# Regrouping the triangular inversions of a delta-rule kernel: groups of 2, 2, 4, 4, 4, 4, 4 chunks instead of 2, 4, 4, 4, 4, 4, 2

## The chip, the core and the metric

The kernel runs on one core of a Trainium2 chip. The metric is the device time of one launch in microseconds; the time before is 1050.36 us, the median of three runs. The engines are TensorE (PE, with PEld for its weight loads), VectorE (DVE), ScalarE (ACT), GpSimd (POOL) and SyncE (SP), whose queue issues all transfers.

## What is computed

A delta-rule attention over 4 batches, 8 heads, 768 tokens and 48 channels is followed by two feed-forward layers over 3072 tokens (384 to 2048 to 384), all in float32.

```python
def _attn_ref(q, k, v, beta):
    k_n = k / (np.linalg.norm(k, axis=-1, keepdims=True) + 1e-06)
    state = np.zeros((B, H, D, D))
    for t in range(S):
        kt, vt, bt = k_n[:, :, t], v[:, :, t], beta[:, :, t, None]
        y[:, :, t] = np.einsum('bhd,bhde->bhe', q[:, :, t], state)
        v_old = np.einsum('bhde,bhd->bhe', state, kt)
        state = state + bt[:, :, :, None] * np.einsum('bhd,bhe->bhde', kt, vt - v_old)
    return y
# layer 1: h = x @ w_in;  g = h if h >= 1, 0 if h <= -1, else (h+1)**2/4;  x = g @ w_out
# layer 2: h = x @ w_in;  g = max(h, 0)**2;                                out = g @ w_out
```

## The kernel before, in words

**Chunks, blocks, units.** The 768 tokens are cut into 24 chunks of 32 tokens; a chunk of all four batches fills 128 partitions. For the feed-forward layers, chunks are joined into blocks (`SIZES` = 2, 2, 3, 3, 3, 3, 3, 2, 3). A unit (L778) is one of 16 slices of 128 of the hidden dimension for one block: the first layer's nine matmuls (`hidden`, L616; three blocks of channels times three products of high and low halves), the relu steps on ScalarE and VectorE (L632 to L647), and, two units later (`LAG` = 2), the second layer's nine matmuls (`out1`). Blocks 0 and 1 have 256 columns, most later ones 384. Units are numbered through: block 0 is units 0 to 15, block 1 units 16 to 31.

**Slots.** Each unit has two slots; slot 2x stands after the first layer of unit x, slot 2x+1 after the second-layer matmuls of unit x-2. `put_a(n, slot, f)` places work ahead of what `put(n, slot, f)` places in the same slot. Every engine runs its own instructions in this written order, so a place in it is a place in the queue of each engine that the work uses.

**Chunk work.** For each chunk, `chunk_steps` gives Ks, Tr, Qs, Ku, Pu and Xt: five groups of 64 small matmuls each (L517 to L568) and a transposition, with a copy or a subtraction after each. Tr multiplies with the inverse of a 32 x 32 triangular matrix. The matrices come from `gram(c)` (L289): 64 matmuls of the chunk's keys with its keys and queries, then a multiplication with a mask (L318). The inversion works on a group of chunks at once, up to four (8 heads times 4 chunks fill the 32 x 32 transpositions). `tri(n, eng)` (L377) gives its parts: `begin`, one transposition by VectorE (L395, some 2.1 us); `pre`, nine small operations for norms and scaling, on ScalarE, VectorE and, for whole matrices, half of the last two on GpSimd (L425, L434), ended by a copy to the diagonal (L435); `steps`, a multiplication and an addition per row (L455, L456), on GpSimd, 30 rows; and `end`, a transposition back by VectorE (L459). There is one buffer for the matrix under inversion (`tx`).

**Groups 0 and 1.** They are inverted by halves (two 16 x 16 triangles, 14 steps), and the off-diagonal part is added on TensorE by `Ld` and `Dld` (`joined`, L468; 64 matmuls for a chunk each, L488 and L496), for which `save` keeps a copy and `rows` (L484) transposes half of the result. Group 0 (chunks 0, 1) is inverted by VectorE in the prologue. Group 1 (chunks 2 to 5) is inverted by GpSimd across the end of the prologue and the first units; grams 2 to 5 stand in the prologue, `rows1` in slot 3, Ld of chunks 2 and 3 in slot 5, `end1` behind it, Ld of chunks 4 and 5 in slot 7, Dld in slots 8 and 24. Chunks 2 and 3 take their chunk steps in slots 9 to 22.

**Later groups.** Group 2 begins with chunk 6: its grams stand in slots 9, 10, 12 and 15. For every group g from 2, `tri_put` (L946) places `begin` one slot after the group's last gram, `pre` three to a slot from the next, the steps from there evenly, and `end` one slot before the first Ks of the group's first chunk. The chunk steps of block n stand evenly in the 32 slots of block n-1, and the grams of the next group go between the steps of a group's first chunk (L922 to L942). That gives, for group 2: begin in slot 16, steps in slots 20 to 45, end in slot 48, first Ks in slot 49. `value(c)` is one GpSimd multiplication per chunk, five slots ahead of its Ks.

**Weights.** Block 0 also makes the weights ready: each of 32 tiles is loaded as 64-bit numbers and turned into two words' high and low halves: two operations of ScalarE (L170, L173, "bits"), one of VectorE (`make`, L180), a cast to the high half (`upper`, L214) and a subtraction for the low half (`lower`, L219). `between(f)` (L727) spreads them over units 0 to 13: two tiles a and b a unit. Tile a's cast is ScalarE's; tile b's is GpSimd's from unit 3. Two weight loads at most are under way, all on SP's queue, with the loads of chunks among them (L805 to L810). `load_kg` loads a gram's keys and queries into a ring of two buffers; the loads of chunks 4 and 5 stand ahead of all weights, those of 6 and 7 after weights 14 and 16.

Of the kernel before, what the change touches and what calls it, by code (L numbers as in the profile page):

```python
# [21 lines left out]
GROUPS = [2, 4, 4, 4, 4, 4, 2]  # L22
# [3 lines left out]
def kernel(  # L26
# [441 lines left out]
    def joined(n):  # L468
        if n == 0:
            l = wp.tile([P, 2, H, T], F32, tag=spare["l"], name="l")  # L470
            z = [wp.tile([P, 2, H, T], F32, tag=spare["z"], name="z")]
            d = wp.tile([P, GC * H, T2], F32, tag=spare["d"], name="d")
        else:
            l = ring.tile([P, GC, H, T], F32, tag="ld", bufs=1, name="l")
            z = [ring.tile([P, 2, H, T], F32, tag="raw", bufs=RAW, name="z") for _ in range(2)]
            d = ring.tile([P, GC * H, T2], F32, tag="raw", bufs=RAW, name="d")
# [250 lines left out]
    def between(f):  # L727
        a, b = tiles[2 * f:2 * f + 2]

        def part(x):  # L730
            if x == 0:
                if a is not None:
                    make(a)
                some(2)
            elif x == 1:
                if a is not None:
                    upper(a, nc.scalar.copy)
                if b is not None:
                    make(b)
                if last_low:  # L740
                    lower(last_low.pop(), V)
            elif x == 2:
                if b is not None:
                    upper(b, G.tensor_copy if f > 2 else nc.scalar.copy)
                    last_low.append(b)
                some(2)
            elif a is not None:
                lower(a, V)

        return part  # L750
# [45 lines left out]
    with tc.manual_schedule():  # L796
# [6 lines left out]
        for c in range(KG):  # L803
            load_kg(KQ + c)
        among = {1: lambda: load_kv(1), 8: lambda: load_kv(HEADS)}  # L805
        for x in range(NW - HELD):
            among.get(x, lambda: None)()
            load_w(order[x])
            if x in (14, 16):
                load_kg(KQ + KG + (x - 14) // 2)  # L810
# [27 lines left out]
        masks += [gram(c, late=2, eng=G) for c in range(KQ, KQ + KG)]  # L838
# [5 lines left out]
        after(value(0), ins)  # L844
        value(1)
        for c in range(HEADS):
            mask_of_head(c)
        go(masks)
# [6 lines left out]
        make(1)  # L855
# [4 lines left out]
        dld0(1)  # L860
        upper(1, nc.scalar.copy)
        whole_bits(4)
        make(2)
        lower(1, V)
        for c in range(GROUPS[1]):
            save1(c)
        upper(2, nc.scalar.copy)
        begin1()
        s0()
        t0()  # L870
        pre1[0]()
        whole_bits(5)
        whole_bits(6)
        s1()
        whole_bits(7)
        t1_()
        go(pre1[1:])
        steps1[0]()
        value(2)
        go(steps1[1:])  # L880
        lower(2, V)
        make(3)
        whole_bits(8)
        upper(3, nc.scalar.copy)
        make(4)
        lower(3, V)
# [4 lines left out]
        x0()  # L891
        upper(4, nc.scalar.copy)
        x1()
        lower(4, V)
        whole_bits(9)
# [13 lines left out]
        put_a(0, 7, lambda: ld1(2), lambda: ld1(3))  # L909
        put_a(0, 8, lambda: dld1(0), lambda: dld1(1))  # L910
        put_a(0, 24, lambda: dld1(2), lambda: dld1(3))
        for c, at_ in ((2, (9, 11, 12, 13, 14, 16)), (3, (15, 17, 18, 19, 20, 22))):
            def steps_of(c=c, box={}):
                if c not in box:
                    box[c] = chunk_steps(c)
                return box[c]
            for i, slot in enumerate(at_):
                put_a(0, slot, lambda i=i, g=steps_of: g()[i]())
# [3 lines left out]
        for c, slot in zip(range(GFIRST[2], GFIRST[3]), (9, 10, 12, 15)):  # L922
            ready[c] = slot
            put_a(0, ready[c], lambda c=c: gram(c))
        for n in range(2, NB):
# [12 lines left out]
            for i, (mark, s_) in enumerate(todo):  # L938
                slot = SL * (n - 1) + i * SL // len(todo)
# [94 lines left out]
```

## Time and profile before

| what | value |
|---|---|
| runs | 1049.24, 1050.36, 1055.89 us |
| the profiled execution | 1048.56 us, span 1046.8 us |
| TensorE busy | 993.8 us, 95% of the span |
| VectorE, ScalarE, GpSimd busy | 582.7, 476.1, 293.3 us |
| mean granted TensorE clock | 0.985 |
| first layer of unit 0 begins | 44.47 us |

The page cuts the span into 40 slices; a digit is tenths. A timeline line gives start, duration, engine, line, operation, tiles written and read, shapes and count; in brackets stands how long the engine had been idle before it and what it waited for. "Issue" is idle time in which the engine waited for nothing that the profile shows.

### The profile page before, as it was taken

What the parts mean: (1) busy time and instruction counts of PE and PEld (TensorE: products, weight loads), DVE (VectorE), ACT (ScalarE), POOL (GpSimd) and SP (SyncE); (2) the same over time, 40 slices, a digit from 0 to 9 for tenths busy, and PEclk for the clock granted to TensorE, in tenths of its full rate; (3) what the DMA queues carried; (4) which work ended last, traced back from release to release, by engine and by line L of the source; (5) the groups of instructions that cost most, each with busy time, mean ns of one, the idle gap of its engine ahead of it and who ended that gap; (6) DMA issues with size and microseconds to landing.
All of it is one profiled execution on the core that took longest, in us unless ns stands there. A gap on an engine that the chain in (4) does not pass through costs nothing.

```text
span 1046.8 us, 33713 instructions
## 1 busy us (share of the span) xinstructions
PE 993.8 (95%) x14824; PEld 949.9 (91%) x14824; DVE 582.7 (56%) x1066; ACT 476.1 (45%) x993; POOL 293.3 (28%) x434
## 2 busy tenths in 40 slices
PE   6669788999999999999999999999999999999998
PEld 5568688898999989999999999999999999999998
DVE  6766965765575566566545677543434343443333
ACT  3756454554554545535445554433333333333332
POOL 3611691492058119419500223110101011010000
PEclk9969899999999999999999999999999999999999
DMA  8776245441541542512111323010101010000000
GB/s 221 223 228 156 64 119 143 110 137 47 154 131 33 172 112 79 145 32 70 32 56 41 94 90 120 2 46 1 46 1 46 1 46 1 23 1 23 1 23 23
DMA packets 36051, 80.93 MB, mean 77 GB/s; under 512 B 4544, under 2 KB 18368, under 8 KB 35904
## 3 DMA queue, kind: packets, MB, share of 16 engines
q1 hardware_dynamic: 35904, 78.78, 25.7%
q8 instruction: 116, 1.90, 0.8%
q14 instruction: 31, 0.25, 0.1%
HBM read 63.03 MB, written 15.73 MB: 75 GB/s over the span
## 4 chain that ended last, share of the span: by engine, by line
PE 82%; DMA 8%; DVE 5%; issue 1%; ACT 1%; SPq 1%; POOL 0%; DVEq 0%; ACTq 0%; POOLq 0%
PE acc L606 36%; PE h L606 36%; DMA raw<-in_w_dram 6%; PE sps L568 2%; PE tr L537 2%; PE yy L523 2%; PE g L302 1%; PE yy L557 1%; PE ks L523 1%; DMA kqt<-in_kq_dram 1%; DVE gl L647 1%; DVE g L633 1%; DVE g L636 1%; DVE wl L180 1%; SPq L129 1%
## 5 line engine op out<-in xcount | busy, mean ns | idle before, releaser
L606 PE MATMUL h<-xh,w 128*128 128x384 f32 (+1 forms) x1632 | 320.3, 332 | 5.3 <-ACT r L632 2.6
L606 PEld LDWEIGHTS h<-xh,w 128*128 128x128 f32 x1632 | 272.4, 190 | 10.1 <-ACT r L632 3.1
L647 DVE TENSOR_TENSOR gl<-g,gh 128x384 fp32r<-128x384 f32 (+1 forms) x272 | 172.3, 633 | 136.8 <-ACT gh L645 131.2
L645 ACT CAST gh<-g 128x384 fp32r<-128x384 f32 (+1 forms) x272 | 134.5, 494 | 208.3 <-DVE g L636 92.9
L606 PE MATMUL h<-xl,w 128*128 128x384 f32 (+1 forms) x816 | 179.3, 328 | 1.3 <-DVE xl L594 1.3
L606 PE MATMUL acc<-gh,w 128*128 128x384 f32 (+1 forms) x864 | 168.5, 331 | 0.8 <-ACT gh L645 0.8
L640 DVE TENSOR_TENSOR g<-r 128x384 f32<-128x384 f32 x128 | 71.3, 557 | 158.5 <-ACT r L639 158.5
L606 PE MATMUL acc<-w,gh 128*128 128x384 f32 x768 | 155.7, 337 | 1.9 <-DVE e L655 1.9
L639 ACT ACTIVATE r<-h,zero 128x384 f32<-128x384 f32 x128 | 74.2, 580 | 167.5 <-PE h L606 167.5
L606 PEld LDWEIGHTS h<-xl,w 128*128 128x128 f32 x816 | 141.0, 190 | 2.0 <-DVE xl L594 2.0
L606 PEld LDWEIGHTS acc<-gh,w 128*128 128x128 f32 x864 | 137.2, 191 | 5.9 <-ACT gh L645 0.9
L606 PEld LDWEIGHTS acc<-w,gh 128*128 128x128 f32 x768 | 136.6, 188 | 2.2 <-ACT gh L645 2.2
L632 ACT ACTIVATE r<-h,one 128x384 f32<-128x384 f32 (+1 forms) x144 | 78.3, 544 | 96.4 <-PE h L606 95.8
L636 DVE SCALAR_TENSOR_TENSOR g<-r,g 128x384 f32<-128x384 f32 (+1 forms) x144 | 89.7, 623 | 42.2 <-ACT g L635 40.5
L633 DVE TENSOR_SCALAR g<-r 128x384 f32<-128x384 f32 (+1 forms) x144 | 60.1, 417 | 86.2 <-ACT r L632 85.1
L455 POOL TENSOR_TENSOR t<-tx,gm 128x58 f32<-128x58 f32 (+9 forms) x164 | 95.7, 583 | 24.2 <-DVE tx L429 8.1
L456 POOL TENSOR_TENSOR tx<-tx,t 128x58 f32<-128x58 f32 (+9 forms) x164 | 97.7, 596 | 12.4
L635 ACT ACTIVATE g<-g 128x384 f32<-128x384 f32 (+1 forms) x144 | 70.2, 488 | 55.0 <-DVE g L633 54.4
L697 POOL CAST xh<-x2r 128x1152 fp32r<-128x1152 f32 x8 | 9.4, 1172 | 293.4 <-PE h L606 246.1
L606 PE MATMUL acc<-gl,w 128*128 128x384 f32 (+1 forms) x432 | 91.3, 320 | 0.0
L606 PE MATMUL acc<-w,gl 128*128 128x384 f32 x384 | 88.1, 337 | 0.0
L606 PEld LDWEIGHTS acc<-gl,w 128*128 128x128 f32 x432 | 72.7, 191 | 0.0
(101 smaller groups left out, 846.7 us busy)
## 6 DMA issues: line engine op xcount, KB each, us to landing
raw<-in_w_dram SPq DMA_DIRECT2D x64, 384.0 KB, 3.8
kqt<-in_kq_dram SPq DMA_DIRECT2D x88, 192.0 KB, 4.1
kv<-in_kv_dram SPq DMA_DIRECT2D x24, 384.0 KB, 3.1
w2f<-wl SPq DMA_DIRECT2D x32, 192.0 KB, 4.0
w2r<-w2f SPq DMA_DIRECT2D x16, 384.0 KB, 3.1
x2r<-x SPq DMA_DIRECT2D x8, 576.0 KB, 4.3
out_dram<-e SPq DMA_DIRECT2D x24, 192.0 KB, 2.0
x<-e SPq DMA_DIRECT2D x18, 192.0 KB, 2.5
```

Source lines behind the costliest of these rows:

```text
L455: eng.tensor_mul(t, by.to_broadcast(shape), of.to_broadcast(shape))
L456: return eng.tensor_add(rest, rest, t)
L523: per_bh(lambda b, h, p, pd: nc.tensor.matmul(o[p, h], kqt[c][pd, b // 2, h, x * T:(x + 1) * T], st[pd, b // 2, h], start=h == 0, stop=x = ...
L606: nc.tensor.matmul(o, *((r, l) if swap else (l, r)), **flags)
L632: marks[0] = nc.scalar.activation(r, h, AF.Relu, bias=one)
L633: marks[1] = nc.vector.tensor_scalar(g, r, 2.0, 0.5, ALU.min, ALU.mult)
L635: nc.scalar.activation(g, g, AF.Square)
L636: nc.vector.scalar_tensor_tensor(g, r, -1.0, g, ALU.add, ALU.max)
L639: marks[0] = nc.scalar.activation(r, h, AF.Relu, bias=zero)
L640: marks[1] = nc.vector.tensor_mul(g, r, r)
L645: nc.scalar.copy(ghi, g)
L647: nc.vector.tensor_sub(glo, g, ghi.bitcast(F32))
```

## The change

Group 1 becomes chunks 2 and 3 alone, group 2 begins with chunk 4 and all later groups shift by two chunks; the last has four. Grams 4 and 5 leave the prologue; grams 4 to 7 stand in slots 1, 3, 9 and 11 of block 0. By the same rules group 2 then has begin in slot 12, steps in slots 16 to 31, end in slot 35, first Ks in slot 36 (the chunk steps of block 2 start four slots into block 1); group 3 has steps from slot 51 and its end in slot 71. Ld and Dld of the second pair of chunks are gone. In the prologue `begin1` and `pre1` stand earlier, the masks of chunks 2 and 3 come before `value(1)`. The loads of chunks 4 to 7 for the grams go among the weight loads. In `between`, both casts are GpSimd's in units 3 to 7 and both ScalarE's elsewhere.

```diff
-GROUPS = [2, 4, 4, 4, 4, 4, 2]
+GROUPS = [2, 2, 4, 4, 4, 4, 4]
...
-            l = ring.tile([P, GC, H, T], F32, tag="ld", bufs=1, name="l")
-            z = [ring.tile([P, 2, H, T], F32, tag="raw", bufs=RAW, name="z") for _ in range(2)]
+            l = ring.tile([P, 2, H, T], F32, tag="ld", bufs=1, name="l")
+            z = [ring.tile([P, 2, H, T], F32, tag="raw", bufs=RAW, name="z")]
...
+        copy = G.tensor_copy if 2 < f < 8 else nc.scalar.copy
...
-                    upper(a, nc.scalar.copy)
+                    upper(a, copy)
...
-                    upper(b, G.tensor_copy if f > 2 else nc.scalar.copy)
+                    upper(b, copy)
...
-        for c in range(KG):
-            load_kg(KQ + c)
-        among = {1: lambda: load_kv(1), 8: lambda: load_kv(HEADS)}
+        among = {
+            1: lambda: load_kv(1), 4: lambda: load_kg(KQ), 6: lambda: load_kg(KQ + 1),
+            8: lambda: load_kv(HEADS), 18: lambda: load_kg(KQ + 2), 20: lambda: load_kg(KQ + 3),
+        }
...
-            if x in (14, 16):
-                load_kg(KQ + KG + (x - 14) // 2)
...
-        masks += [gram(c, late=2, eng=G) for c in range(KQ, KQ + KG)]
...
+        go(masks)
         value(1)
         for c in range(HEADS):
             mask_of_head(c)
-        go(masks)
...
         make(0)
-        make(1)
+        begin1()
         whole_bits(3)
         upper(0, nc.scalar.copy)
         lower(0, V)
         dld0(0)
         dld0(1)
+        pre1[0]()
+        go(pre1[1:])
+        steps1[0]()
+        make(1)
...
+        value(2)
+        go(steps1[1:])
         whole_bits(7)
         t1_()
-        go(pre1[1:])
-        steps1[0]()
-        value(2)
-        go(steps1[1:])
...
         put_a(0, 5, lambda: ld1(0), lambda: ld1(1))
-        put_a(0, 7, lambda: ld1(2), lambda: ld1(3))
-        put_a(0, 8, lambda: dld1(0), lambda: dld1(1))
-        put_a(0, 24, lambda: dld1(2), lambda: dld1(3))
-        for c, at_ in ((2, (9, 11, 12, 13, 14, 16)), (3, (15, 17, 18, 19, 20, 22))):
+        put_a(0, 7, lambda: dld1(0), lambda: dld1(1))
+        for c, at_ in ((2, (9, 10, 12, 13, 14, 16)), (3, (15, 17, 18, 19, 20, 22))):
...
-        for c, slot in zip(range(GFIRST[2], GFIRST[3]), (9, 10, 12, 15)):
+        for c, slot in zip(range(GFIRST[2], GFIRST[3]), (1, 3, 9, 11)):
...
-                slot = SL * (n - 1) + i * SL // len(todo)
+                o = 4 if n == 2 else 0
+                slot = SL * (n - 1) + o + i * (SL - o) // len(todo)
```

## Rows read from the trace of the kernel before

**Rows 1.** The page, part 2: granted TensorE clock in 40 slices, in tenths.
```profile
PEclk9969899999999999999999999999999999999999
```

**Rows 2.** Windows of block 1 and after: length, engines' busy us, clock, DMA share, GB/s.
```profile
131.61:192.84 61.23, 56.01 (x1514) 51.48 (x1514) 36.18 (x71) 30.15 (x73) 26.56 (x43) 1.00 0.46 125
192.84:264.00 71.16, 69.78 (x1338) 63.95 (x1337) 47.59 (x84) 37.73 (x79) 41.78 (x66) 1.00 0.34 97
```

**Rows 3.** Waits of TensorE from 44 to 210 us: total, times, longest.
```profile
PE z L488 <- DVE g L633: 6.1, 1, 6.1
PE xt L591 <- ACT kv L561: 5.7, 2, 4.1
```

**Rows 4.** Timeline, end of group 1's inversion: VectorE, GpSimd, TensorE.
```profile
56.08 1.05 DVE L484 STREAM_TRANSPOSE d<-tx 128x512 f32<-128x512 f32 x1 [0.48 <-POOL tx L456]
...
55.78 0.26 POOL L456 TENSOR_TENSOR tx<-tx,t 128x28 f32<-128x28 f32 x1
...
57.27 1.90 PE L488 MATMUL z<-d,l 32*32 32x16 f32 x128 [6.11 <-DVE g L633]
```

**Rows 5.** Timeline of TensorE, prologue, Tr of chunk 0.
```profile
33.41 1.01 PE L537 MATMUL tr<-kv,gp 32*32 32x48 f32 x36 [2.56 <-issue]
```

**Rows 6.** Timeline of TensorE, units 3 to 6, and one gram's mask on VectorE.
```profile
64.74 0.98 PE L488 MATMUL z<-d,l 32*32 32x16 f32 x94
66.08 0.46 PE L488 MATMUL z<-d,l 32*32 32x16 f32 x34 [0.37 <-issue]
66.47 0.98 PE L606 MATMUL h<-xh,w 128*128 128x256 f32 x6
67.29 0.52 PE L606 MATMUL h<-xl,w 128*128 128x256 f32 x3
67.73 0.96 PE L496 MATMUL w<-gp,z 32*32 32x16 f32 x84
71.93 0.82 PE L496 MATMUL w<-gp,z 32*32 32x16 f32 x44 [3.24 <-issue]
...
82.40 0.95 PE L606 MATMUL h<-xh,w 128*128 128x256 f32 x6
...
78.18 0.69 DVE L318 TENSOR_TENSOR gp<-g,mask 128x512 f32<-128x512 f32 x1 [1.15 <-PE g L302]
```

**Rows 7.** Timeline: first layer of unit 8, then group 2's preparation, first and last step.
```profile
96.35 0.98 PE L606 MATMUL h<-xh,w 128*128 128x256 f32 x6
...
112.39 0.20 DVE L435 COPY tx<-st 128x32 f32<-128x32 f32 x1 [0.51 <-POOL tx L434]
...
114.94 0.41 POOL L455 TENSOR_TENSOR t<-tx,gm 128x30 f32<-128x30 f32 x1
...
160.14 0.26 POOL L456 TENSOR_TENSOR tx<-tx,t 128x30 f32<-128x30 f32 x1
```

**Rows 8.** Timeline of GpSimd, first and last step of group 5.
```profile
390.01 0.24 POOL L455 TENSOR_TENSOR t<-tx,gm 128x30 f32<-128x30 f32 x1 [1.14 <-DVE tx L434]
...
430.36 0.46 POOL L456 TENSOR_TENSOR tx<-tx,t 128x30 f32<-128x30 f32 x1
```

**Rows 9.** Timeline: end of group 2 on VectorE; TensorE: Tr after it, Pu of chunk 4.
```profile
165.15 2.22 DVE L459 STREAM_TRANSPOSE gp<-tx 128x1024 f32<-128x1024 f32 x1
...
169.57 0.88 PE L537 MATMUL tr<-kv,gp 32*32 32x48 f32 x64 [1.82 <-DVE kv L533]
...
142.84 0.88 PE L557 MATMUL yy<-kv,gp 32*32 32x48 f32 x64
```

**Rows 10.** Timeline of TensorE: a second layer after 4.1 us idle; Xt of chunk 4.
```profile
114.77 1.63 PE L606 MATMUL acc<-gh,w 128*128 128x256 f32 x6
...
147.76 0.55 PE L591 MATMUL xt<-ident,kv 128*128 128x128 f32 x3 [1.61 <-ACT kv L561]
```

**Rows 11.** Gram 7 on TensorE; the weight casts (ns min/median/max, first and last start).
```profile
79.30 1.10 PE L302 MATMUL g<-kqt 48*32 48x64 f32 x64
80.33 0.97 PE L606 MATMUL acc<-gh,w 128*128 128x256 f32 x6
...
L214 ACT CAST w<-wl x22: 494/511/519, 27.2 to 126.2; 128x384 fp32r<-128x384 f32 x22
L214 POOL CAST w<-wl x10: 704/718/827, 64.2 to 122.7; 128x384 fp32r<-128x384 f32 x10
```

More of the change, by code (lines that the diff above doesn't have):

```diff
@@ L860 @@
         dld0(1)
+        pre1[0]()
+        go(pre1[1:])
+        steps1[0]()
+        make(1)
         upper(1, nc.scalar.copy)
-        whole_bits(4)
-        make(2)
-        lower(1, V)
         for c in range(GROUPS[1]):
             save1(c)
-        upper(2, nc.scalar.copy)
-        begin1()
+        whole_bits(4)
+        lower(1, V)
         s0()
         t0()
-        pre1[0]()
         whole_bits(5)
@@ L874 @@
         s1()
+        value(2)
+        go(steps1[1:])
         whole_bits(7)
         t1_()
-        go(pre1[1:])
-        steps1[0]()
-        value(2)
-        go(steps1[1:])
+        make(2)
+        whole_bits(8)
+        upper(2, nc.scalar.copy)
+        make(3)
         lower(2, V)
[L882 to L886, printed above, removed]
         q1()
@@ L891 @@
         x0()
+        upper(3, nc.scalar.copy)
+        make(4)
+        x1()
+        lower(3, V)
         upper(4, nc.scalar.copy)
-        x1()
+        whole_bits(9)
         lower(4, V)
-        whole_bits(9)
         whole_bits(10)
```

## The prediction

> **What bounds the kernel now.** I read the page first. The granted clock is full in almost all of the 40 slices and falls only near the start [rows 1], and the windows after block 1 show TensorE busy for 69.78 of 71.16 us [rows 2]. So from there on TensorE is the bound, and every microsecond it idles or runs at the lower clock counts one for one. What can be won lies before: in block 1 TensorE is busy for 56.01 of 61.23 us [rows 2], and earlier it idles more. The view of waits, for TensorE from 44 to 210 us, names the two largest [rows 3]: 6.1 us before the first Ld matmuls of group 1, and 5.7 us in two waits of the transposition xt, 4.1 the longer. Then the timeline shows who is late at each.
>
> The first wait looks like the gain of this change: GpSimd ends the inversion of group 1 at 55.78 + 0.26 = 56.04, VectorE's transposition of its rows (L484) starts at 56.08, TensorE's Ld at 57.27 [rows 4]. But the same row says that VectorE had waited only 0.48 us for GpSimd. It was itself busy until 56.08 - 0.48 = 55.6 with the conversions and relu steps of units 0 and 1. An inversion that ends six microseconds sooner moves this place by half a microsecond and no more.
>
> **The change, part by part.** The sum is made against the profiled execution's own 1048.56 us (span 1046.8, 1.76 around it). The median of the three runs is 1050.36, so 1.8 us more; a difference within 1% (10.5 us) is about what a measurement of this kernel cannot tell from no change.
>
> *Prologue: 0.* Grams 4 and 5, two saves and the GpSimd masks of chunks 4 and 5 leave it; the inversion of group 1 begins earlier. The first layer of unit 0 hangs on another chain, inversion of group 0, Ld, Dld, chunk steps 0 and 1, and the grams stood in a time in which TensorE waits for that inversion. The stall of 2.56 us inside tr of chunk 0 [rows 5] lies on it. I count it as staying: two grams are 128 matmuls, and two such stalls, at 66.08 and 71.93, have 34 + 9 + 84 = 127 between them [rows 6], so the next ones fall on the same instructions as before. Bounds: -2.6 (the stall goes) to +1 (one more weight cast of 0.51 us on ScalarE [rows 11] ahead of unit 0, and its wait).
>
> *Units 0 to 5: -5.* Added ahead of L484 on VectorE: the masks of grams 4 and 5, 0.69 each [rows 6], less the 0.48 that it waited: +0.9. Removed: Ld of two chunks, 64.74 to 66.47, 1.73 us [rows 6]; part of the 3.24 us stall that ends at 71.93 [rows 6], because the Dld now stands half a unit earlier and the work between is less dense; and part of the half-rate time after it. Fully taken that is 0.9 - 1.7 - 3.2 = -4.1, and with 2 us of slow clock -6.2; I take -5. Grams 4 and 5 themselves run while TensorE waits for VectorE anyway. Bounds: -0.8 (only the Ld goes) to -9 (also the whole first wait). So unit 6 starts its first layer at 77.4 instead of 82.40 [rows 6].
>
> A row and a rule differ here. The 3.24 us are "issue": nothing that the profile shows was waited for. The Trainium skill, "Runtime: NRT & Kernel Launch", section "Instruction fetch mechanics", says that an engine's instructions come in blocks of 256, the next fetched while the current one runs, so that a boundary is mostly hidden. The spacing fits such blocks (a matmul and its weight load are two instructions), the hiding does not. By the rule nothing would stall again and this term would be -9, by the rows -5.
>
> *Group 2 on GpSimd: the new wait.* This is the part that decides. Today the gram of the last chunk of the group stands just before the first layer of unit 8 (96.35); VectorE has the last preparation at 112.59 (L435), and GpSimd steps from 114.94 to 160.40 [rows 7], with two weight casts among them. The end is due in slot 48, unit 24. After the change the same chain hangs on unit 6: last gram in slot 11, begin in slot 12, steps from slot 16, end in slot 35, first Ks in slot 36. The distance from that first layer to the last preparation is 112.59 - 96.35 = 16.2 us. No casts are in the way any more, since units 8 and later cast on ScalarE. The 30 steps took 40.8 us from 390.01 to 430.82 [rows 8] with one value product, so 41.5 with what else is issued beside them. End possible at 77.4 + 16.2 + 41.5 = 135.1.
>
> When would the others reach the end in slot 35? From the first layer of unit 6 at 82.40 to Ku of chunk 4 done, at 142.84, the old kernel took 60.4 us [rows 6, 9]. In that stretch two grams go (2.1), Dld of two chunks with its wait (some 3, an estimate from the 1.73 of their Ld), and the four steps of chunk 4 come behind the end (3.5): 51.8 us, so at 77.4 + 51.8 = 129.2. VectorE stands there 6 us before GpSimd is done. It waits in order, so all later relu steps wait behind it, then the Ks subtraction of chunk 4, and TensorE at the Tr of chunk 4. From the start of the end's transposition to a Tr took 165.15 to 169.57, 4.4 us [rows 9]; Tr, Qs and Ku are three more steps of about 0.87. So at 135.1 + 4.4 + 2.6 = 142.1 the kernel is where the old one was at 142.84 (first layers up to unit 18, Ku of chunk 4) [rows 9]: -0.7. Of the 5 us won and of ten slots' earlier start almost nothing is left; TensorE idles some 10 us.
>
> *Clock after it: +2.* After the 4.1 us wait of xt [rows 3] six matmuls of a second layer took 1.63 us [rows 10], against 0.95 for six of the same size at the full clock [rows 6]; that is 1.0 lost in a layer of nine matmuls, and some two layers pass before the clock is back. Bounds 0 to 3.
>
> *Block 1 afterwards: -3.4.* The end of group 2 no longer stands in front of Tr of chunk 6 (1.82 us of idle [rows 9]), and the wait of xt at 147.76 (1.61 us [rows 10]) falls into the time in which TensorE is held anyway. Bounds -3.4 to 0.
>
> *Two grams later: +2.1.* Blocks 2 and later have twelve grams where they had ten; one takes 1.03 us of TensorE (79.30 to 80.33 [rows 11]), and there TensorE is full. Nothing hides it. Bounds 2.1 to 2.3.
>
> *Group 3: +1.* Its steps stand from slot 51, its end in slot 71. At 61.23/16 = 3.83 us a unit in block 1 and about 4.1 in block 2 (71.16 us for some 17 units [rows 2]) that is 6.5 x 3.83 + 3.5 x 4.1 = 39 us, for 41 to 42 of GpSimd. It is late by 2 to 3 us; a unit's two layers cover most. Bounds 0 to 6. Groups 4 to 6 have 23 or more slots, 47 us: nothing.
>
> *Casts: 0.* The condition 2 < f < 8 takes units 3 to 7, five units and ten tiles; ten are on GpSimd today too [rows 11], spread over units 3 to 12. They move to a time in which GpSimd is idle, and ScalarE, which is then rid of them, gains 0.51 us a unit [rows 11]. Units 8 and 9 get two casts beside their weight bits; should ScalarE set the pace there, it costs 0.51 a unit.
>
> *Loads: 0.* The gram loads go behind weights 4, 6, 18 and 20 on SP's queue. The last two wait for buffers that grams 4 and 5 free in units 0 and 1, before the queue is there. The bytes are the same. The loads of grams 8 and 9 leave block 0. Bounds -0.6 to +2.
>
> Sum: -0.7 + 2 - 3.4 + 2.1 + 1 = +1.0, so 1049.6 us.
>
> **The rivals.** *A, the early gain stays.* The stall of 3.24 and more of the first wait go, the term of units 0 to 5 is -9, unit 6 starts at 73.4 and the end of group 2 is possible at 131.1: 1045.6, and 1043 with less slow clock. For it: VectorE's conversions of units 0 and 1 then no longer run beside GpSimd's steps. Against: VectorE's busy time before L484 and the two added masks. The page's rule named above leads here too.
>
> *B, the short window of group 3 decides, slower.* Place: VectorE's wait at slot 71. If GpSimd begins its steps only 2 us later than counted (value products and the preparation stand before it), VectorE is held for 5 us, the transposition and the way to Tr add 4.4, and the clock falls once more, 2: 9 to 11 instead of +1, about 1058. It decides as soon as the lateness exceeds what two layers cover, some 4 us. For it: 39 us against 41.5. Against: an end stands in the window after block 1 too, where TensorE idles 1.4 us in all [rows 2]; but there GpSimd had 29 slots.
>
> *C, nothing of it is on the path:* the wait of group 2 is not there because units 8 to 17 take 42 us or more. Then TensorE is not idle but slowed by as much; 1046 to 1052, and the time does not tell it from the forecast.
>
> **How the numbers follow.** Forecast with C 0.50, A 0.25, B 0.20, other 0.05. The range reaches from 1041 (A with the bound of the prologue) to 1060 (B), with little beyond. Faster by over 1% would need 1039.9: a part of A and of "other", 0.13. Slower by over 1%, from 1060.9: a part of B and "other", 0.12. Within: 0.75.
>
> **What would show it.** Right: L484 starts near 57, not near 50; the Ld follows it; unit 6 begins near 77; GpSimd steps group 2 from about 94 to 135; VectorE's transposition of the end (L459) is released by GpSimd, and TensorE's longest wait is Tr of chunk 4, 9 us or more, followed by a stretch at 1.2 GHz. Wrong: no wait for GpSimd at the end of group 2, steps in under 38 us, or a longer wait at group 3 than at group 2.

## The result, and the profile after

The changed kernel takes 1061.16 us, the median of six runs (1060.06 to 1066.14), against 1050.92 for six runs of the kernel before: a ratio of 1.0102, with a 95% interval of 1.0071 to 1.0132. It is slower by 1%. The prediction was 1049.6 with a range of 1041 to 1060: wrong in the number, in the sign and, by a little, in the range. The profiled execution took 1061.56 us (span 1059.8), so 13.0 more than that of before (by medians it is 10.2); the steps below are counted against these 13.0, the experiments by medians.

The page, parts 2 and 4: the granted clock, and the chain that ended last.

```profile
PEclk9988879999999999999999999999999999999999
...
PE 83%; DVE 8%; POOL 3%; issue 3%; ACT 2%; DMA 0%; SPq 0%; DVEq 0%; ACTq 0%; POOLq 0%
```

The clock is lower in slices 4 and 6 than in [rows 1] (8 and 7 against 9 and 9) and higher in slice 3 (8 against 6). GpSimd, which holds 0% of the chain on the page of the kernel before, now holds 3%.

Windows of the kernel after, cut at the first layers of units 0 and 6, at Tr of chunk 4 and at the end of block 1; the columns are those of [rows 2], VectorE's busy time being the third of the five.

```profile
47.48:81.52 34.04, 27.11 (x858) 24.42 (x858) 25.07 (x53) 24.79 (x59) 4.25 (x8) 0.85 0.62 194
81.52:147.47 65.95, 48.27 (x823) 43.64 (x817) 56.93 (x96) 32.93 (x80) 45.92 (x70) 0.83 0.38 102
147.47:198.69 51.22, 50.23 (x1396) 46.16 (x1396) 30.02 (x65) 24.40 (x59) 21.00 (x35) 0.95 0.42 119
```

The second window is where the time goes: TensorE works 48.27 of 65.95 us, at a mean clock of 0.83, and VectorE is busy for 56.93 of them. For the kernel before, the nearest window, from unit 6 to the start of Pu of chunk 4, shows:

```profile
82.40:142.84 60.44, 49.23 (x1272) 44.93 (x1264) 47.67 (x97) 32.43 (x80) 32.51 (x48) 0.92 0.36 95
```

There VectorE had 47.67 us of work with 97 instructions; now it has 56.93 with 96. The kinds are nearly the same, so the instructions became dearer. TensorE, on the other hand, runs 823 matmuls where it ran 1272: part of its work has moved behind this window.

Waits of TensorE in the kernel after, from 44 to 215 us (total, times, longest), to be held against [rows 3]:

```profile
PE yy L557 <- issue: 5.0, 2, 3.7
PE tr L537 <- DVE gp L459: 4.7, 1, 4.7
PE g L302 <- DVE gp L318: 3.9, 1, 3.9
...
PE xt L591 <- ACT kv L561: 1.1, 1, 1.1
```

The two waits of [rows 3] are gone or small. In their place stand the end of group 2 (L459), gram 5 waiting for gram 4's mask, and an issue stall of 3.7 us.

The first layers show where the 13.0 us arise (starts in us, from the timelines of TensorE in both profiles):

| first layer of unit | before | after | difference |
|---|---|---|---|
| 0 | 44.47 | 47.48 | +3.0 |
| 6 | 82.40 | 81.52 | -0.9 |
| 18 | 139.58 | 139.45 | -0.1 |
| 19 | 143.66 | 148.91 | +5.3 |
| 20 | 148.13 | 154.68 | +6.6 |
| 36 | 210.59 | 215.61 | +5.0 |
| 38 | 218.34 | 229.44 | +11.1 |
| 96 | 473.42 | 486.46 | +13.0 |

Three places lose: the prologue (3.0), the end of group 2 between units 18 and 20 (6.7), and the end of group 3 between units 36 and 38 (6.1). Units 0 to 5 win 3.9. Not all of the 6.7 and 6.1 is waiting: in both places the kernel after also runs two steps more, with one Xt less (in units 36 and 37 a Tr and a gram): some 1.5 us each time, an estimate from 0.82 us for a step, 1.03 for a gram and 0.3 for the Xt at the full clock.

**The prologue.** Timeline of the kernel after: VectorE, ScalarE and TensorE.

```profile
33.48 0.69 DVE L429 TENSOR_TENSOR tx<-gm,st 128x512 f32<-128x512 f32 x1
34.21 0.20 DVE L435 COPY tx<-st 128x32 f32<-128x32 f32 x1
...
34.43 0.52 DVE L180 SCALAR_TENSOR_TENSOR wl<-raw 128x384 int32<-128x384 int32 x1
35.03 0.51 ACT L214 CAST w<-wl 128x384 fp32r<-128x384 f32 x1 [5.70 <-DVE wl L180]
...
36.94 0.46 ACT L545 COPY u<-tr 128x384 f32<-128x384 f32 x1
```

The preparation of group 1 (to L435) now stands ahead of `make(1)` (L180) on VectorE. ScalarE comes to the cast of tile 1 early, waits 5.70 us for it, and behind the cast stand two saves, the bits of one tile and the copy of u of chunk 0, which starts at 36.94 instead of 34.46 in the kernel before. That is the way to unit 0.

**The end of group 2.** Timeline, to be held against [rows 4, 6, 7 and 9]: group 1's last step and its transposition; then unit 6, the stall, the last preparation, the first and last step of group 2, the end, and Tr of chunk 4.

```profile
47.88 0.27 POOL L456 TENSOR_TENSOR tx<-tx,t 128x28 f32<-128x28 f32 x1
...
59.20 1.05 DVE L484 STREAM_TRANSPOSE d<-tx 128x512 f32<-128x512 f32 x1
...
81.52 0.97 PE L606 MATMUL h<-xh,w 128*128 128x256 f32 x6
...
91.16 1.01 PE L557 MATMUL yy<-kv,gp 32*32 32x48 f32 x36 [3.66 <-issue]
...
99.17 0.21 DVE L435 COPY tx<-st 128x32 f32<-128x32 f32 x1 [0.51 <-POOL tx L434]
...
99.09 0.23 POOL L455 TENSOR_TENSOR t<-tx,gm 128x30 f32<-128x30 f32 x1
...
143.49 0.32 POOL L456 TENSOR_TENSOR tx<-tx,t 128x30 f32<-128x30 f32 x1
...
144.95 0.55 DVE L533 TENSOR_TENSOR kv<-kv,ks 128x384 f32<-128x384 f32 x1
145.42 2.00 DVE L459 STREAM_TRANSPOSE gp<-tx 128x1024 f32<-128x1024 f32 x1
...
147.47 1.50 PE L537 MATMUL tr<-kv,gp 32*32 32x48 f32 x64 [4.73 <-DVE gp L459]
148.91 1.65 PE L606 MATMUL h<-xh,w 128*128 128x256 f32 x6
```

The prologue's gain for group 1 is there (done at 48.15 instead of 56.04), and L484 makes nothing of it. For group 2, GpSimd is done at 143.81, VectorE begins the end at 145.42 with no idle time before it, and TensorE, which has waited 4.73 us, then runs at the lower of its two levels: 64 matmuls in 1.50 us, where [rows 9] has 0.88. That VectorE arrives so late has its reason mainly in its own instructions, which get slower, and in part in the order of its queue. The code holds every engine to the written order only in block 0 (L797); from unit 16 on it holds TensorE alone (L975). So VectorE's Ks subtraction of chunk 4 (L533, slot 36) runs here ahead of the end (L459, slot 35). Groups of VectorE's instructions between 99 and 130 us (busy us, mean ns, then idle before), kernel before:

```profile
L219 DVE TENSOR_TENSOR w<-wl,w 128x384 fp32r<-128x384 f32 x12 | 7.9, 661 | 0.0
L180 DVE SCALAR_TENSOR_TENSOR wl<-raw 128x384 int32<-128x384 int32 x11 | 6.7, 608 | 0.0
L633 DVE TENSOR_SCALAR g<-r 128x256 f32<-128x256 f32 x6 | 2.4, 395 | 0.7 <-ACT r L632 0.7
```

and kernel after:

```profile
L219 DVE TENSOR_TENSOR w<-wl,w 128x384 fp32r<-128x384 f32 x12 | 10.9, 909 | 0.0
L180 DVE SCALAR_TENSOR_TENSOR wl<-raw 128x384 int32<-128x384 int32 x11 | 8.9, 809 | 0.0
L633 DVE TENSOR_SCALAR g<-r 128x256 f32<-128x256 f32 x7 | 4.0, 565 | 0.0
```

The kernel before shows the same effect within one run. There GpSimd's steps begin at 114.94 [rows 7]; the subtraction L219 from 99 to 115 us, and from 115 to 130 us:

```profile
L219 DVE TENSOR_TENSOR w<-wl,w 128x384 fp32r<-128x384 f32 x5 | 2.7, 550 | 0.0
L219 DVE TENSOR_TENSOR w<-wl,w 128x384 fp32r<-128x384 f32 x7 | 5.2, 741 | 0.0
```

**The end of group 3.** Timeline of the kernel after, VectorE and TensorE:

```profile
218.98 2.12 DVE L459 STREAM_TRANSPOSE gp<-tx 128x1024 f32<-128x1024 f32 x1 [3.02 <-POOL tx L456]
...
222.59 1.31 PE L606 MATMUL h<-xh,w 128*128 128x384 f32 x6 [2.55 <-ACT r L632]
...
224.77 1.50 PE L537 MATMUL tr<-kv,gp 32*32 32x48 f32 x64
226.20 1.76 PE L606 MATMUL acc<-gh,w 128*128 128x384 f32 x6
```

VectorE stands 3.02 us before the end of GpSimd's steps; the relu step behind it on VectorE comes late, TensorE misses its matmuls by 2.55 us, and Tr and the second layer follow at the lower clock (1.50 and 1.76 us; the same second layer took 1.32 at the full clock two units earlier). With the moved Tr and gram that makes the 6 us.

### The profile page after: what moved, and what is told of

The parts are those of the page before. It is cut to its first block, busy times and chain, and to the rows that moved or that the text cites. A ratio compares the mean times of both kernels' runs of the same rounds, so it can differ in the third digit from the quotient of the medians.

```text
span 1059.8 us, 33190 instructions
## 1 busy us (share of the span) xinstructions
PE 997.2 (94%) x14568; PEld 951.7 (90%) x14568; DVE 583.0 (55%) x1066; ACT 474.9 (45%) x987; POOL 286.6 (27%) x431
## 4 chain that ended last, share of the span: by engine, by line
PE 83%; DVE 8%; POOL 3%; issue 3%; ACT 2%; DMA 0%; SPq 0%; DVEq 0%; ACTq 0%; POOLq 0%
PE acc L606 36%; PE h L606 36%; PE tr L537 2%; PE sps L568 2%; PE g L302 2%; PE yy L557 2%; PE yy L523 2%; PE ks L523 1%; POOL tx L456 1%; POOL t L455 1%; DVE gl L647 1%; DVE g L636 1%; DVE w L219 1%; DVE wl L180 1%; DVE g L633 1%
## 5 line engine op out<-in xcount | busy, mean ns | idle before, releaser
L606 PE MATMUL h<-xh,w 128*128 128x384 f32 (+1 forms) x1632 | 324.3, 335 | 5.8 <-ACT r L632 4.8
L606 PEld LDWEIGHTS h<-xh,w 128*128 128x128 f32 x1632 | 275.2, 192 | 11.5 <-ACT r L632 5.7
L633 DVE TENSOR_SCALAR g<-r 128x384 f32<-128x384 f32 (+1 forms) x144 | 60.1, 417 | 98.0 <-ACT r L632 97.5
L278 POOL TENSOR_TENSOR kv<-kv,nt 128x384 f32<-128x384 f32 x24 | 22.6, 942 | 234.0 <-DMA kv<-in_kv_dram 130.9
```

Source lines behind the costliest of these rows:

```text
L606: nc.tensor.matmul(o, *((r, l) if swap else (l, r)), **flags)
L633: marks[1] = nc.vector.tensor_scalar(g, r, 2.0, 0.5, ALU.min, ALU.mult)
```

## The experiments

The theory at their start: the new waits at the ends of groups 2 and 3 make the loss, with a part from the prologue. The rivals: the prologue alone shifts everything; the conversions of VectorE, slowed by GpSimd's steps, are the bound and the waits only their sign; the casts or the regrouping itself cost. Unless said otherwise, an edit is made to the changed kernel.

**1. `make(1)` ahead of the preparation of group 1.**

```diff
         dld0(1)
+        make(1)
         pre1[0]()
...
-        make(1)
         upper(1, nc.scalar.copy)
```

> The changed kernel with one line moved in the prologue: VectorE's make of weight tile 1 stands ahead of the preparation of group 1's inversion instead of behind it. Theory: the 3.0 us by which unit 0 starts later (47.48 against 44.47) come from ScalarE, which waits 5.7 us in order for that tile and so copies u of chunk 0 late (36.94 against 34.46). Then the copy starts near 34, unit 0 near 45, and the time is 2 to 3 us under the changed kernel's 1061.2, about 1058.5. Rival: the start is set by the instruction stalls of TensorE; then unit 0 still starts past 47 and the time stays at 1061.

Measured: 1061.79 us, ratio to before 1.0118 (1.0094 to 1.0143): nothing gained. The wait of ScalarE fell from 5.70 to 2.54 us and the copy of u came at 35.26, 1.7 earlier, but the issue stall in Tr before it had grown from 1.74 to 2.84 us, and unit 0 began only 0.6 earlier (46.84). Unit 6 began 1.5 later (82.98): one issue stall of 2.21 us stands between them where the kernel after has 1.41 and 1.18, and the granted clock from 70 to 83 us is 0.74 instead of 0.87. The end of group 2:

```profile
143.92 0.26 POOL L456 TENSOR_TENSOR tx<-tx,t 128x30 f32<-128x30 f32 x1
144.22 1.99 DVE L459 STREAM_TRANSPOSE gp<-tx 128x1024 f32<-128x1024 f32 x1 [3.35 <-POOL tx L456]
```

Here VectorE does wait for GpSimd: it is free from 140.87, although its conversions are as slow as in the kernel after (0.910 us for L219), because here the end stands ahead of the Ks subtraction and of relu steps of units 17 and 18 in its queue. Unit 19 began at 148.41 against 148.91, so by these two runs this order is worth no more than half a microsecond. The theory missed; the time is the rival's, with unit 0 at 46.84 between what the two expected. The cast wait of the prologue is real, but what it frees is taken back.

**2. Group 3's end later.** The chunk steps of block 3 begin four slots into block 2, as those of block 2 do in block 1.

```diff
-                o = 4 if n == 2 else 0
+                o = 4 if n in (2, 3) else 0
```

> The changed kernel with the chunk steps of block 3 starting four slots later, so that the end of group 3 stands some 3 to 4 slots (7 us) later. Theory: TensorE's loss of 6 us between units 36 and 38 is VectorE's wait of 3.0 us for GpSimd at the end of group 3, with the 2.1 us transposition and the queue behind it. Then that wait is gone and the time is 4 to 6 us under 1061.2, about 1056. Rival: the loss there is the transposition and the evacuations of block 1 alone, whoever is ready first; then the time stays within 1 us of 1061.

Measured: 1057.08 us, 4.1 less than the kernel after (ratio to before 1.007, 1.0048 to 1.0092). The end stands at 221.07 with no wait before it, and unit 38 begins at 222.72 instead of 229.44. As expected: the short window of group 3 costs some 4 us, and only the rest is left. The intervals of the two kernels overlap a little; the traces are clearer, with units 36 and 37 taking 8.61 us instead of 13.83.

**3. Group 2 without its steps.** Of 30 steps one is left; the inversion of group 2 is thus mostly not computed.

```diff
-            for i, s_ in enumerate(steps):
+            for i, s_ in enumerate(steps if g > 2 else steps[:1]):
```

> The changed kernel without 29 of the 30 inversion steps of group 2 on GpSimd (that part of the computation is left out). Theory: VectorE's weight conversions in units 8 to 13 take 0.9 to 1.05 us each instead of 0.55 because GpSimd's steps run beside them, and so VectorE reaches the end of group 2 (slot 35) only at 145.4. Without the steps the conversions take 0.55 to 0.6 and the end's transposition starts near 130 (15 us sooner); the time falls by 12 to 16 us, to 1046 to 1049. Rival: units 8 to 17 are paced by TensorE and ScalarE; then the conversions shorten but the transposition still starts past 140 and the time falls by less than 5 us.

Measured in a single run: 1040.8 us, 20.4 less than the kernel after, more than the 12 to 16 expected. VectorE's conversions were fast again and the end came 20 us earlier (125.77). VectorE's groups, 99 to 126 us:

```profile
L219 DVE TENSOR_TENSOR w<-wl,w 128x384 fp32r<-128x384 f32 x12 | 6.6, 551 | 0.0
L180 DVE SCALAR_TENSOR_TENSOR wl<-raw 128x384 int32<-128x384 int32 x10 | 6.1, 614 | 0.0
```

Unit 19 began at 130.31, 18.6 before that of the kernel after. The stretch before the end of group 2 hangs on GpSimd's steps, then; but by their end, or by what they do to VectorE? Experiment 5 parts the two.

**4. The casts alone**, in the kernel before.

```diff
+        copy = G.tensor_copy if 2 < f < 8 else nc.scalar.copy
...
-                    upper(a, nc.scalar.copy)
+                    upper(a, copy)
...
-                    upper(b, G.tensor_copy if f > 2 else nc.scalar.copy)
+                    upper(b, copy)
```

> The kernel before with the rule of the casts alone: both casts of units 3 to 7 by GpSimd, both by ScalarE in units 8 to 12. Theory: ten casts are on GpSimd either way and none sets the end; within 1.5 us of the kernel before. Rival: the casts that leave the stretch of group 2's inversion relieve GpSimd and VectorE there; 2 to 4 us faster than before.

Measured: 1050.69 us, ratio 0.9996 (0.9977 to 1.0015). Nothing, as expected.

**5. Memsets in place of group 2's steps 2 to 29**: two memsets for each step, which only write and read nothing. The inversion of group 2 is thus left out.

```diff
+            if g == 2:
+                def still():
+                    G.memset(gm2[0], 0.0)
+                    G.memset(gm2[0][:, 0:15], 0.0)
+                steps = steps[:1] + [still] * (len(steps) - 2) + steps[-1:]
```

> The changed kernel with 28 of the 30 steps of group 2 replaced by GpSimd memsets of about the same length (1.4 us a step; that part of the inversion is left out). GpSimd is as long occupied, but reads no operands. Theory: it is GpSimd's reading of operands beside VectorE's two-operand conversions that makes these 0.8 to 0.9 us instead of 0.55; with memsets they take 0.55, VectorE stands at the end of group 2 near 128 and waits there for GpSimd until 135 to 142. So the time falls by 2 to 8 us only, to 1053 to 1059, where it fell by 20 without the steps. Rival: any work on GpSimd slows VectorE as much; then the conversions stay at 0.8 to 0.9 and the time at 1059 to 1062.

Measured in a single run: 1064.24 us. The number missed, since the memsets took longer than the steps that they stand for: 100.68 to 149.19, 48.5 us against 44.7. But the two causes came apart. VectorE's groups, 99 to 130 us, and the end of group 2 (lines are two higher here):

```profile
L219 DVE TENSOR_TENSOR w<-wl,w 128x384 fp32r<-128x384 f32 x12 | 7.2, 604 | 0.0
L180 DVE SCALAR_TENSOR_TENSOR wl<-raw 128x384 int32<-128x384 int32 x11 | 6.7, 608 | 0.0
```

```profile
148.67 0.56 DVE L535 TENSOR_TENSOR kv<-kv,ks 128x384 f32<-128x384 f32 x1 [10.74 <-POOL kv L278]
149.22 2.02 DVE L461 STREAM_TRANSPOSE gp<-tx 128x1024 f32<-128x1024 f32 x1
151.29 1.50 PE L539 MATMUL tr<-kv,gp 32*32 32x48 f32 x64 [14.97 <-DVE gp L461]
```

With GpSimd only writing, VectorE is not slowed (0.604 against 0.909 us), reaches the Ks subtraction 10.74 us before GpSimd gives it the value product, and TensorE waits 14.97 us. With the steps, VectorE is slow and TensorE waits 4.73. Units 6 to 17 show VectorE's part without the end: from the first layer of unit 6 to that of unit 18 it takes 57.93 us in the kernel after, 48.94 here and 44.92 without the steps. There are two bounds of nearly equal length: GpSimd's chain, and VectorE's own work while that chain runs. Taking away VectorE's slowness leaves the chain: begun at 100.68, with 44.7 us as in the kernel after it would end at 145.4 (an estimate), and in the kernel after the end stands at 145.42.

**6. The windows as late as before.** The regrouping stays; group 2 begins in slot 16 and ends in slot 45, the grams of group 3 stand in slots 33 to 42, and group 3 begins and ends later too. It has the edit of experiment 1 as well.

```diff
+        for c, slot in zip(range(GFIRST[3], GFIRST[4]), (33, 36, 39, 42)):
+            ready[c] = slot
+            put_a(0, ready[c], lambda c=c: gram(c))
...
-                if j == 0 and 2 <= g < NG - 1:
+                if j == 0 and 3 <= g < NG - 1:
...
-                o = 4 if n == 2 else 0
+                o = {2: 14, 3: 6}.get(n, 0)
...
+            a = max(a, {2: 15, 3: 46}.get(g, 0))
```

> The changed kernel with group 2's inversion begun in slot 16 and its end in slot 45, as in the kernel before (there 16 and 48), the chunk steps of block 2 in the last 18 slots of block 1, group 3's grams in slots 33 to 42, its begin in slot 47 and its end some five slots later than now; make of tile 1 early as in the first experiment. Theory: both short windows cost, the first through conversions beside GpSimd's steps and the wait behind them, the second through the wait. With room in both the time is 8 to 13 us under the changed kernel, 1048 to 1053. Rival: the loss comes with the regrouping itself (two more grams after block 1, the prologue); then it stays above 1056.

Measured: 1051.42 us, ratio to before 1.0006 (0.9986 to 1.0026). All 10 us are back, as expected. So the regrouping as such costs nothing that is left at the end. Slowed conversions alone are not the loss either: from 99 to 130 us L219 still takes 0.818 us on average here, against 0.661 in the kernel before. How the 10 us divide among the parts of this edit is not shown: unit 0 begins at 45.27 here, 2.2 us before that of the kernel after, and experiment 1, with the same prologue, gained nothing.

**7. The casts undone** in the changed kernel: tile a's cast by ScalarE, tile b's by GpSimd from unit 3 on.

```diff
-                    upper(a, copy)
+                    upper(a, nc.scalar.copy)
...
-                    upper(b, copy)
+                    upper(b, G.tensor_copy if f > 2 else nc.scalar.copy)
```

> The changed kernel with the casts as in the kernel before: tile b's cast by GpSimd in units 3 to 12. Theory: five casts of 0.72 to 0.83 us then stand among group 2's steps and lengthen GpSimd's 44.7 us to 48 or 49; the end of group 2 is 3 to 4 us later, the time 2 to 4 us above the changed kernel, 1063 to 1065. Rival: GpSimd's length is hidden behind VectorE's pace there; within 1 us of 1061.

Measured: 1067.39 us, ratio to before 1.0153 (1.0133 to 1.0173), so 6.2 more than the kernel after; the direction was right, the size larger than expected. The steps began at 104.73 (99.09 in the kernel after) and lasted to 151.07, 46.3 us against 44.7. Tr of chunk 4:

```profile
153.18 1.50 PE L537 MATMUL tr<-kv,gp 32*32 32x48 f32 x64 [7.60 <-DVE gp L459]
```

TensorE waits 2.9 us longer there than in the kernel after, so time of GpSimd does count in the changed kernel. But not all of the 6 us is shown to be the casts': unit 0 begins 1.8 us later (49.31), before any cast that this edit moves, and unit 6 3.0 us later. More than half of the later begin of the steps is there by then; the steps themselves grew by 1.6 us, not by the 3 to 4 expected.

**8. Both ends later still.**

```diff
-                o = 4 if n == 2 else 0
+                o = 10 if n in (2, 3) else 0
```

> The changed kernel with the chunk steps of blocks 2 and 3 starting ten slots late instead of four and none, so that both ends stand 6 and 7 to 8 slots later. Theory: TensorE's wait of 4.7 us at Tr of chunk 4 and its half-rate clock after it go (some 5 us), and the wait at the end of group 3 as in the second experiment (4); but the slow units 8 to 15 stay. 1051 to 1054. Rival: the first end is not what holds TensorE, units 8 to 17 are slow anyway and the chunk work is only shifted; then only group 3's part comes back, 1056 to 1058.

Measured: 1057.58 us, ratio to before 1.0065 (1.0044 to 1.0085), the same as experiment 2, so the rival held. Tr of chunk 4 waits next to nothing:

```profile
150.55 2.16 DVE L459 STREAM_TRANSPOSE gp<-tx 128x1024 f32<-128x1024 f32 x1
...
153.83 0.88 PE L537 MATMUL tr<-kv,gp 32*32 32x48 f32 x64 [0.19 <-DVE kv L533]
```

Unit 20 was level with the kernel before (147.69 against 148.13), and unit 32 was 7.9 us behind it (200.75 against 192.84): between the two TensorE works 49.82 us instead of 41.62, with 1443 matmuls instead of 1121. The chunk work that was moved out of the wait's way is paid for in the slots into which it is pushed. The profiled execution is the slowest of the six (1061.73) and begins unit 0 at 49.52. Experiment 6, which moves the ends about as far and the begins too, is 6 us faster by medians; of the 9.9 us between the two profiled executions some 4 are there at unit 0, and why is open.

**9 and 10. More room after experiment 6**, to see whether a version beats both kernels: the ends some slots later again, and the begin of group 2 two slots earlier in the first and as in experiment 6 in the second.

```diff
-                o = {2: 14, 3: 6}.get(n, 0)
+                o = {2: 18, 3: 8}.get(n, 0)
...
-            a = max(a, {2: 15, 3: 46}.get(g, 0))
+            a = max(a, {2: 13, 3: 46}.get(g, 0))
```

> As in the kernel with windows as late as before, but the chunk steps of blocks 2 and 3 start 18 and 8 slots into the block (14 and 6 there), so that the end of group 2 stands two to four slots later, and its begin stands two slots earlier. Theory (what was left of the loss sits at the end of group 2, where Tr of chunk 4 waited 3.6 us and its xt 3.3, and the early stretch gains 4): both waits fall under 1 us, the time is 1046 to 1049. Rival (as with the ends moved later: VectorE's own work in units 8 to 17 holds TensorE all the same, and the shifted chunk work is only paid later): 1050 to 1053.

> The same with the begin of group 2 left in slot 16, where the weights are nearly done. Theory: no more of GpSimd's steps run beside VectorE's weight conversions than before, the end is as late as in the kernel before, 1047 to 1050. Rival: 1050 to 1053, as in the run above; if this one is faster than the one above by 1.5 us or more, it is the overlap of steps and conversions that costs, and not the wait.

Measured: 1053.34 us (ratio 1.0029, 1.0008 to 1.0050) and 1053.81 (1.0023, 1.0001 to 1.0046). (The change of `a` belongs to the first of the two.) The theory failed in both, and the times lie a little over the rival's upper end; the begin makes no difference. The second one is the plainest picture of a deferred cost. Its first layer of unit 24 begins at 152.53, 10.6 us ahead of the kernel before (163.11). Windows of units 24 to 31 and of units 40 to 59 in it:

```profile
152.53:195.87 43.34, 36.96 (x1115) 32.95 (x1113) 23.97 (x51) 17.45 (x41) 30.43 (x52) 0.92 0.29 77
228.38:322.31 93.93, 92.84 (x2108) 84.02 (x2101) 57.45 (x99) 44.80 (x94) 40.50 (x66) 1.00 0.41 116
```

and in the kernel before:

```profile
163.11:192.84 29.73, 27.75 (x729) 25.66 (x727) 16.22 (x32) 12.45 (x30) 0.83 (x1) 1.00 0.43 116
226.62:314.74 88.12, 87.40 (x1781) 79.94 (x1780) 52.45 (x98) 44.12 (x91) 30.77 (x53) 1.00 0.39 115
```

The eight units 24 to 31 take 43.34 us in place of 29.73, with 36.96 us of TensorE's work in place of 27.75 (more small matmuls of chunks, and part of it at the lower clock) and 6.4 us without work in place of 2.0, and units 40 to 59 another 5.8 us, nearly all of it TensorE's own work (92.84 against 87.40). No version that was run beats the kernel before.

## Why the prediction was wrong, point by point

Its places were right: the gain at the start is eaten before and at the end of group 2, and group 3 comes on top. Its mechanism at the end of group 2 was right in part only. Two of its three signs of being wrong came true: VectorE had no idle time for GpSimd at the end of group 2, and its wait at group 3 (3.02 us) was the longer one. What failed are three steps: the prologue at 0, the end of group 2 priced as a wait of a VectorE that runs at its old speed, and the cover of group 3. Nearly all errors lie to the same side. By its own steps, with the table of first layers:

| step | predicted | measured |
|---|---|---|
| prologue | 0 | +3.0 |
| units 0 to 5 | -5 | -3.9 |
| unit 6 to unit 20: end of group 2, with the clock after it | +4.7 | +7.4 |
| units 20 to 36 | -1.8 | -1.5 |
| units 36 and 37: end of group 3 | +1 | +6.1 |
| from unit 38 on: two grams more | +2.1 | +1.9 |
| sum | +1.0 | +13.0 |

(The third line as predicted: the state at -0.7 after -5 was won means 4.3 lost on the way, then 2 of clock, less the xt wait of 1.6 us that goes, which lies before unit 20 [rows 10]. The 1.8 of the fourth line are the other part of the -3.4. The forecast of 1049.6 starts from the profiled execution; from the median before it would be 1051.4.)

The measured lines follow the place, not the kind of work. Up to unit 18 the two kernels are level. From unit 18 to unit 96 TensorE works 335.21 us with 7275 matmuls in the kernel after, against 326.65 us with 6956, and it is idle for 11.8 us against 7.2. The difference is five steps of 64 matmuls, two grams and Ks, Tr and Qs of chunk 4, some 4.5 us by the durations above; the rest of the longer work is mostly the lower clock behind the two waits. The kernel before ran these five steps in units 6 to 17, which take 57.18 us there and 57.93 in the kernel after. The prediction had counted the moved steps, as 2.1 for the grams and 2.6 for three steps; what it had too small is the idle time and the clock.

*"Prologue: 0", bounds to +1: failed.* The term looked at TensorE's stalls and not at the queue of VectorE, past which the preparation of group 1 was moved. One line of that queue holds ScalarE for 5.70 us. Experiment 1 shows the wait, and that shortening it gives no time at the end; what makes unit 0 begin anywhere between 44.7 and 49.5 us in kernels with nearly this prologue (experiments 8 and 10) stays open: issue stalls are part of it, they shift with every edit, and with one profile of each kernel it is not known how far they shift from run to run.

*Units 0 to 5: 1 us short, and not made of the parts that were counted.* The reading that the inversion is not what holds L484 held: GpSimd is done at 48.15, and L484 still begins only at 59.20, with no idle time before it. The Ld follows at 61.78. The stalls hardly went: those for issue add up to 3.0 us in units 0 to 5, against 3.6 before.

*The end of group 2: right place, wrong sizes within it.* Counted was a last preparation 16.2 us after unit 6 and steps of 41.5 us, with the end of GpSimd at 135.1. Measured are 17.9 (99.38 less 81.52, with an issue stall of 3.66 in it) and 44.7, of which 3.0 are three value products where one was counted; with unit 6 4.1 us later that makes 143.81. The other miss is that VectorE was counted as waiting there from 129.2, and it arrives at 145.42. For the end itself this is worth 1.6 us, since GpSimd is done only at 143.81; but it takes the wait out of one place and spreads it over units 13 to 17. The stretch was priced with the old kernel's instructions, and in the old kernel the steps began late, when the conversions of the weights were nearly over. Begun at 99, they run beside the conversions of units 9 to 15, and VectorE's instructions with two inputs there take 0.81 and 0.91 us in place of 0.55 to 0.66. The trace of the kernel before had this price in it: 0.550 us before the steps begin, 0.741 beside them. Experiments 3 and 5 show this effect and the chain of GpSimd as two bounds side by side. The condition of rival C came about (units 8 to 17 took 43.7 us, 95.75 to 139.45, and VectorE did not wait for GpSimd), but TensorE waited all the same, since the end stands ahead of Tr. The "some 10 us" in which TensorE idles were 4.7 at Tr and 6.8 in short waits for ScalarE and VectorE between 118 and 133 us, in units 13 to 16:

```profile
118.55 0.62 PE L606 MATMUL acc<-gl,w 128*128 128x256 f32 x3 [1.12 <-DVE gl L647]
...
122.46 0.97 PE L606 MATMUL acc<-gh,w 128*128 128x256 f32 x6 [1.80 <-ACT gh L645]
...
132.39 1.65 PE L606 MATMUL h<-xh,w 128*128 128x256 f32 x6 [2.20 <-ACT r L632]
```

The Trainium skill, "SBUF — State Buffer", section "Who interferes with whom", says that a VectorE instruction with two inputs in SBUF contends with a GpSimd instruction that reads SBUF, and not with one that only writes it. Experiment 5 agrees: 0.604 us beside memsets, 0.909 beside the steps. The relu step L633 has one input and was slowed as well (0.395 in the kernel before, 0.565 after).

*Block 1 afterwards: held.* The wait in front of Tr of chunk 6 is gone, and from Tr of chunk 4 to the end of block 1 TensorE works 50.23 of 51.22 us.

*Group 3: +1, late by 2 to 3 us, of which a unit's two layers cover most: failed.* VectorE stood 3.02 us at it, quite as counted. The cover was not there: behind VectorE's wait stand the transposition (2.12 us) and then the relu step of the unit, so TensorE is without work for 2.55 us and then at half its rate. Experiment 2 puts the price at 4.1 us by medians, which agrees with the 6.1 of the table less some 1.5 for the moved Tr and gram. It is below the 9 to 11 of rival B, with its mechanism.

*Casts 0, loads 0: held* (experiment 4 for the casts; no wait for a load shows on TensorE), but the casts only in the kernel before. Within the changed kernel undoing them costs up to 6.2 us (experiment 7), of which a longer wait of 2.9 at Tr of chunk 4 is shown.

*Two grams +2.1: the sum fits by luck.* The windows from unit 38 to unit 96, kernel before and kernel after:

```profile
218.34:473.42 255.08, 253.25 (x5175) 231.77 (x5175) 158.80 (x282) 127.81 (x264) 110.21 (x179) 1.00 0.35 102
229.44:486.46 257.02, 253.48 (x5180) 232.17 (x5174) 157.31 (x281) 127.62 (x262) 113.55 (x180) 1.00 0.36 103
```

TensorE does the same work in both; what is longer is its idle time, by 1.7 us. Tr waits there for the Ks subtraction, 2.8 us in three waits against 1.0 in one, which "Groups 4 to 6: nothing" had left out. The moved grams were paid for earlier, in units 18 to 37.

The range failed for a reason of its own. The bounds of the single terms went far enough, but for the prologue's (+1, where +3.0 was measured); rival B was priced alone, on a forecast in which everything before it held, so its 1058 was an upper end; the prologue and group 2 lay on the same side as it. And the 1% that the prediction held for the limit of what can be told was too wide: with six runs of each kernel the interval is 0.7 to 1.3%, clear of no change.

## What to carry to other kernels

When work is moved to an earlier place beside an engine that it slows (0.55 us alone and 0.91 beside it, here), price the instructions there anew: durations from a stretch where the two did not overlap do not hold. Starting a chain earlier by shortening the window that it has, and by putting it beside the busiest stretch of another engine, was no gain here; ask what it will then run beside and who stands waiting behind its end. Small matmuls that leave a stretch in which TensorE waits anyway are paid for where it is full. And before work is held to be free in a prologue, walk every in-order queue that it is moved past, not only that of the engine that bounds the kernel.

## What the runs showed of the hardware

- VectorE beside GpSimd's multiplications and additions: 128 x 384 operations with two inputs take 0.81 to 0.91 us on average, beside GpSimd's memsets 0.60 to 0.61, without steps 0.55 to 0.61.
- A GpSimd memset of 128 x 1024 float32 took 0.961 us and one of 128 x 480 took 0.503, so a fill takes 0.94 to 1.05 ns a column. The steps' multiplication of 128 x 240 took 0.812 us, 3.4 ns a column.
- Stalls for issue on TensorE move with the program: 3.66 us at 91 us in the kernel after, 1.47 in the same matmuls after the edit of experiment 1, which has 2.21 at 67 us where the kernel after has 1.41. Between 66 and 91 us of the kernel after they stand 127, 128 or 254 matmuls apart, each with its weight load: between the stalls that end at 66.32 and 70.15 there are 25 + 9 + 94.
